# A decode step on one core: the wait for the two final stores moves from SyncE to GpSimd

## The chip, the cores and the metric

The kernel runs on one core of a Trainium2 chip. The metric is the device time in microseconds, the median of several runs. One more execution was taken by the hardware profiler; durations below are from that execution. The engines are called as in the profile: PE (matmuls; PEld its weight loads), DVE (vector), ACT (scalar), POOL (GpSimd) and SP (SyncE). A q behind a name (SPq) marks the engine's sequencer, which issues transfers and waits on semaphores.

## What is computed

One token for each of two batch rows is taken through a normalisation, windowed attention over a cache and a gate from a small dense network:

```
xn = layernorm(x)                                  # 2 x 1 x 448
q = xn @ wq                                        # 16 heads of 256
k, v = last 2048 rows of the caches                # 8 heads, each serves two of q
o = softmax(q k^T / 16) v
s = o @ wo                                         # back to 448
g = silu(relu(xn @ w1) @ w2)
out = x + s * g                                    # 2 x 1 x 448, bf16
```

## The kernel before

A small class, `_Prog`, holds one list of operations for each engine. Every operation names those that it depends on. `op` (L31) adds an engine instruction and `dma` (L38) adds a transfer, issued by the engine named (`e.dma_start`, L39). `run` (L43) then gives each transfer a semaphore of its own, which its completion raises by 16, and each engine one semaphore that its instructions raise by 1 where somebody depends on them. `emit` (L60) writes an engine's list in order; ahead of an operation it writes `eng.wait_ge` (L69) for each semaphore that the operation depends on and that this engine hasn't waited for yet. An operation whose function is `None` is made of its waits alone.

An engine runs its list strictly in order. What each list holds:

- SP issues all the large loads: `wq`, `w1`, `w2`, four tiles of the key cache of 4 MB each, later the value cache into the same four tiles, then `wo` in five parts. At the end it issues the first half of the result.
- ACT issues the three small loads of `x`, then clears accumulators and makes the exponentials; at the end it issues the second half of the result.
- POOL clears small tiles and builds an identity matrix in the first three microseconds (`p_xc`, `i0`, `p_id`, `p_z`, L249 to L269). It has no operation after that, and it issues no transfer.
- DVE transposes the keys within each tile, takes the maxima and turns the probabilities; PE makes the products. Both have jumps written into their code, which set the order in which their code is fetched (`emit_dve`, `emit_pe`).

The four pairs of batch row and head group are worked through in turn: transposed keys, scores, softmax, then the products with the values; the output projection with `wo` closes. At the end, the sum `v_t` (L546) multiplies the projection by the gate, and `v_o` (L548) adds `x` and leaves the result in `out_sb`, four rows from partition 0 and four from partition 32. `d_o` (L550) stores these two halves, the first issued by SP, the second by ACT; each moves 4 rows of 224 bytes to memory. L551 then makes SP wait until both have landed, and L552 makes PE wait for `v_o`. Nothing else follows in any list.

Of the kernel before, what the change touches and what calls it, by code (L numbers as in the profile page):

```python
# [11 lines left out]
PE, DVE, ACTE, SP, POOL = "pe", "dve", "act", "sp", "pool"  # L12
# [121 lines left out]
def bass_recurrent_scan__sliding_block_cached__dense_activation_relu__decode_kernel(  # L134
# [34 lines left out]
    with es:  # L169
        pr = _Prog(nc, es)  # L170
# [70 lines left out]
        def half(t, h):  # L241
            return t.rearrange("b s (k h n) -> h (b s k) n", h=2, n=NCOL)[h]
# [305 lines left out]
        v_o = pr.op(DVE, lambda e: e.tensor_tensor(  # L548
            out=out_sb[0:ROWS, :], in0=tmp[0:ROWS, :], in1=x_c[0:ROWS, :], op=ALU.add), [v_t] + d_xc)
        d_o = [pr.dma(eng, half(out, h), out_sb[32 * h:32 * h + 4, :], [v_o]) for h, eng in ((0, SP), (1, ACTE))]  # L550
        pr.op(SP, None, d_o)  # L551
        pr.op(PE, None, [v_o])  # L552

        pr.run()
# [28 lines left out]
```

## Time and profile before

| | |
|---|---|
| median of three runs | 110.05 us (110.00 to 110.17) |
| the profiled execution's own time | 110.12 us |
| its span, from the first to the last instruction | 108.8 us |
| mean granted TensorE clock | 0.843 |
| bytes read, mean rate | 44.11 MB, 405 GB/s |
| busy: DVE, PE, PEld, ACT, POOL | 61.5, 58.9, 15.7, 9.0, 2.1 us |
| last instruction of POOL | starts at 2.66 us, 0.23 us long |
| last sum (L548) | starts at 107.12 us, 0.27 us long |
| issue of the two stores (L39) | 107.42 us; 0.35 us on SP, 0.27 us on ACT |
| SP's wait for the stores (L69) | 1.0 us |

The span covers the kernel's instructions; the time of an execution also holds what lies around them, here 1.32 us. Waits are not counted as busy. Where a view of the profile names a releaser, it is the operation whose semaphore came last. Line numbers are those of the kernel; since one helper writes all transfers and another all waits, these have the lines of the helpers, L39 and L69.

### The profile page before, as it was taken

To read this page: it belongs to the slowest core of one execution; us is meant where nothing else is said; L and a number is where in the kernel's file an instruction comes from. 1 tells how busy PE (TensorE), PEld (TensorE's weight loads), DVE (VectorE), ACT (ScalarE), POOL (GpSimd) and SP (SyncE) were. 2 spreads that over 40 slices of the span, in tenths; PEclk is the share of its full clock that TensorE was granted. 3 is DMA by queue.
4 is the path that set the end of the run, shared out by engine and by line. 5 is a ranking of instruction groups with operands and counts; after the bars stand their busy time and mean duration, and the time that the engine had idled before them with its cause. 6 is when DMAs were issued, how large, how long until landed. Compare 5 with 4: busy or idle time off the path is not lost.

```text
span 108.8 us, 1117 instructions
## 1 busy us (share of the span) xinstructions
PE 58.9 (54%) x469; PEld 15.7 (14%) x469; DVE 61.5 (57%) x84; ACT 9.0 (8%) x18; POOL 2.1 (2%) x13
## 2 busy tenths in 40 slices
PE   0001295650000069929961995299448967869672
PEld 0000023120000012101200120011033222303131
DVE  2920007644099979999999999940448332204021
ACT  2970000000000000002000200020020000000000
POOL 7000000000000000000000000000000000000000
PEclk9999999995555558995997599679955699999999
DMA  6899999999998999899989998999899899999960
GB/s 165 337 449 390 413 434 486 423 398 494 434 410 386 506 434 410 386 482 458 410 386 482 458 410 386 482 458 410 386 482 458 367 416 428 434 428 448 376 242 1
DMA packets 2487, 44.16 MB, mean 406 GB/s; under 512 B 306, under 2 KB 436, under 8 KB 820
## 3 DMA queue, kind: packets, MB, share of 16 engines
q1 hardware_dynamic: 2456, 44.11, 95.0%
q8 instruction: 3, 0.05, 0.2%
q10 hardware_dynamic: 28, 0.00, 0.0%
HBM read 44.11 MB, written 0.00 MB: 405 GB/s over the span
## 4 chain that ended last, share of the span: by engine, by line
DMA 56%; DVE 28%; PE 8%; SPq 5%; issue 1%
DMA kv<-in_A_k_cache_dram 32%; DVE kv L346 24%; DMA wqo<-in_A_wo_dram 23%; PE sbk L311 7%; SPq L39 5%; PE fbk L311 1%; DVE q_x L375 1%; DVE rm L363 1%; DVE rm_t L365 0%; DVE bias L369 0%; DVE bt L366 0%; DVE tmp L546 0%; DVE out_sb L548 0%
## 5 line engine op out<-in xcount | busy, mean ns | idle before, releaser
L311 PE MATMUL sbk<-kv,qstat 128*8 128x512 bf16 x128 | 30.1, 1086 | 22.8 <-DVE kv L346 22.8
L346 DVE STREAM_TRANSPOSE kv<-kv 128x2048 f32<-128x2048 f32 x16 | 35.6, 2274 | 4.6 <-DMA kv<-in_A_k_cache_dram 4.6
L311 PEld LDWEIGHTS sbk<-kv,qstat 128*8 128x8 bf16 x128 | 5.2, 107 | 46.1 <-DVE kv L346 28.8
L311 PE MATMUL obk<-kv,pt 128*16 128x512 bf16 x128 | 9.5, 441 | 2.6 <-DVE xg L427 1.2
L424 DVE TENSOR_SCALAR o_odd<-obk,rs 128x256 f32<-128x256 f32 x4 | 1.9, 484 | 11.1 <-PE obk L311 11.1
L370 ACT ACTIVATE e_sb<-sbk,bias 128x512 bf16<-128x512 f32 x4 | 2.8, 688 | 51.8 <-DVE bias L369 51.8
L311 PE MATMUL sbk<-kv,f 128*8 128x512 f32 x14 | 7.0, 613 | 0.0
L311 PE MATMUL qbk<-wqo,xr 128*4 128x512 bf16 x28 | 3.2, 626 | 4.2 <-DMA wqo<-in_A_wq_dram 4.2
L363 DVE TENSOR_REDUCE rm<-sbk 128x1 f32<-128x512 f32 x4 | 2.6, 662 | 4.7 <-PE sbk L311 4.7
L311 PE MATMUL mbk<-ident,xg 2*128 2x2 bf16 x7 | 0.3, 161 | 8.4 <-issue 8.4
L329 DVE TENSOR_SCALAR q_x<-qbk 128x512 bf16<-128x512 f32 x1 | 0.7, 691 | 7.2 <-PE qbk L311 7.2
L311 PEld LDWEIGHTS obk<-kv,pt 128*16 128x16 bf16 x128 | 3.2, 97 | 8.7 <-issue 5.0
L375 DVE STREAM_TRANSPOSE q_x<-e_sb 128x512 bf16<-128x512 bf16 x4 | 2.8, 691 | 1.7 <-ACT e_sb L370 1.7
L392 DVE TENSOR_TENSOR pt<-spk,pmask 128x512 bf16<-128x512 f32 x4 | 2.6, 684 | 0.8 <-PE spk L311 0.8
L311 PE MATMUL qbk<-w_sb,xr 128*2 128x448 bf16 x28 | 2.8, 572 | 0.0
L528 DVE COPY wc<-wbk 128x448 f32<-128x448 f32 x1 | 0.6, 624 | 3.8 <-PE wbk L311 3.8
L311 PE MATMUL spk<-q_x,perm 128*32 128x128 bf16 x16 | 0.7, 298 | 3.1 <-DVE q_x L375 3.1
L340 DVE CAST qstat<-mbk 32x256 bf16<-32x256 f32 x4 | 1.7, 420 | 0.7 <-PE mbk L311 0.7
L427 DVE SCALAR_TENSOR_TENSOR xg<-obk,rs,o_odd 128x256 bf16<-128x256 f32 x4 | 1.9, 484 | 0.1
L311 PE MATMUL wbk<-wqo,at 128*2 128x448 bf16 x24 | 1.4, 352 | 1.0 <-DMA wqo<-in_A_wo_dram 1.0
L271 DVE BATCH_NORM_STATS2 st<-x_sb 2x6 f32<-2x448 bf16 x1 | 0.6, 616 | 2.0 <-DMA x_sb<-in_A_x_dram 2.0
L311 PEld LDWEIGHTS sbk<-kv,f 128*8 128x8 f32 x14 | 1.3, 96 | 3.1 <-issue 2.6
(72 smaller groups left out, 33.0 us busy)
## 6 DMA issues: line engine op xcount, KB each, us to landing
kv<-in_A_k_cache_dram SPq DMA_DIRECT2D x4, 4096.0 KB, 39.5
kv<-in_A_v_cache_dram SPq DMA_DIRECT2D x3, 4096.0 KB, 22.1
kv<-in_A_v_cache_dram SPq DMA_DIRECT2D x2, 2048.0 KB, 17.6
wqo<-in_A_wq_dram SPq DMA_DIRECT2D x1, 3584.0 KB, 12.2
w_sb<-in_B_w_dram SPq DMA_DIRECT2D x2, 1568.0 KB, 17.1
wqo<-in_A_wo_dram SPq DMA_DIRECT2D x1, 2240.0 KB, 24.4
wqo<-in_A_wo_dram SPq DMA_DIRECT2D x2, 448.0 KB, 25.2
wqo<-in_A_wo_dram SPq DMA_DIRECT2D x1, 336.0 KB, 25.9
```

What stands on the lines that cost most here:

```text
L39: o = _Op(eng, lambda e: e.dma_start(dst, src), [d for d in deps if d is not None], True)
L271: v_bn = pr.op(DVE, lambda e: e.bn_stats(st6[0:B, :], x_sb[0:B, :]), [d_x])
L311: return lambda e: e.matmul(out_ap, lhsT=lhsT, rhs=rhs, start=start, stop=stop, skip_group_check=True, **kw)
L329: v_q = pr.op(DVE, lambda e: e.tensor_scalar(out=view(q_x, 0, [[256, 8], [128, 2], [1, 32]]), in0=view(qbk, 0, [[64, 8], [1, 2], [2, 32]]) ...
L340: st["q"] = st["mbk"] = pr.op(DVE, lambda e, Q=Q: e.tensor_copy(qstat[32 * Q:32 * Q + 32, 256 * Q:256 * Q + 256], mbk[32 * Q:32 * Q + 32, ...
L346: st["turn", u] = pr.op(DVE, lambda e, n=n: e.transpose(kf[:, 2048 * n:2048 * n + 2048], kf[:, 2048 * n:2048 * n + 2048]), [d_k[u]])
L363: v = pr.op(DVE, lambda e: e.tensor_reduce(out=rm[:, 0:1], in_=sbk[u % 2][:, :], axis=AX.X, op=ALU.max), [last_S[u], p_z, st.get(("rmt", u ...
L370: st["exp", u] = pr.op(ACTE, lambda e: e.activation(e_sb[:, :], sbk[u % 2][:, :], ACT.Exp, bias=bias[:, 0:1], accum_out=ssum[:, u:u + 1]), ...
L375: st["et", u] = pr.op(DVE, lambda e: e.transpose(q_x[:, 512 * u:512 * u + 512], e_sb[:, :]), [st["exp", u], m_qt])
L392: st["pt", u] = pr.op(DVE, lambda e: e.tensor_tensor(out=view(pt[u], 0, [[8, 64], [2, 4], [1, 2]]), in0=view(spk, 128 * u, [[2, 64], [0, 4 ...
L424: v = pr.op(DVE, lambda e: e.tensor_scalar(out=o_odd[:, :], in0=obk[:, DH:2 * DH], scalar1=rs[:, 2 * u + 1:2 * u + 2], scalar2=None, op0=A ...
L427: st["osb", u] = pr.op(DVE, lambda e: e.scalar_tensor_tensor(out=o_sb[:, lo:lo + DH], in0=obk[:, 0:DH], scalar=rs[:, 2 * u:2 * u + 1], in1 ...
```

## The change

The operation that waits for both stores moves from SP's list to POOL's. The stores themselves stay where they are, one issued by SP and one by ACT, and PE's wait stays too.

```diff
         d_o = [pr.dma(eng, half(out, h), out_sb[32 * h:32 * h + 4, :], [v_o]) for h, eng in ((0, SP), (1, ACTE))]
-        pr.op(SP, None, d_o)
+        pr.op(POOL, None, d_o)
         pr.op(PE, None, [v_o])
```

In `run`, this makes `emit` write the waits for the two stores' semaphores as the last of POOL's code, behind the clearing of `at2`, and SP's code ends with the issue of its store.

## The prediction

> **What bounds the kernel, and its end.** I read the page's shares and the chain first, to see whether the change lies where time is spent. The chain that ended last is transfers and vector work from front to back:
>
> ```profile
> span 108.8 us, 1117 instructions
> ...
> DMA 56%; DVE 28%; PE 8%; SPq 5%; issue 1%
> ```
>
> The DMA engines carry 95% of the span (queue q1), and nothing of that is edited. The change is at the tail only, so the second view is the order of time from 106.7 us on (start, length, what):
>
> ```profile
> 107.12 0.27 DVE L548 TENSOR_TENSOR out_sb<-tmp,x_c 36x112 bf16<-36x112 f32 x1
> 107.42 0.35 SPq L39 DMA_DIRECT2D out_dram<-out_sb  x1
> 107.42 0.27 ACTq L39 DMA_DIRECT2D out_dram<-out_sb  x1
> ```
>
> The last sum is ready at 107.39, both stores are issued at 107.42, and nothing is listed after that. Yet the span runs to 108.80: what is left is SP's wait. The third view is what SP waited for, and the fourth the instructions of the wait's line:
>
> ```profile
> SPq L69 <- DMA out_dram<-out_sb: 1.0, 1, 1.0
> ```
> ```profile
> L69 PEldq EVENT_SEMAPHORE  x10: 51/51/4097, 8.3 to 107.4; - x10
> L69 DVEq EVENT_SEMAPHORE  x3: 21/21/50, 3.3 to 106.8; - x3
> L69 SPq EVENT_SEMAPHORE  x1: 192/192/192, 108.6 to 108.6; - x1
> ```
>
> SP's wait is one instruction for both stores' semaphores. Its record starts at 108.604, after the ACT store's last arrival (108.588), and ends at 108.796, 23 ns after the SP store's (108.773). That is the end of the span. The profiled execution took 110.12 us, so 1.32 us lie outside the 108.80; its own 110.12 stands 0.07 above the median of 110.05.
>
> What fills the time behind the span is seen in the trace's list of semaphore updates. The kernel's own semaphores are numbers 99 to 125. Number 2 is not the kernel's; it is raised nine times in each of four groups, here in us from the span's start:
>
> ```
> a  -8.361  -3.592  -2.699  -2.656  -2.632  -2.520  -2.481  -2.447  -2.397
> b  -0.371  -0.336  -0.298  -0.254  -0.231  -0.119  -0.081  -0.046   0.000
> c 107.893 108.048 108.086 108.130 108.923 108.968 109.006 109.040 109.087
> d 109.872 109.906 109.944 109.988 110.012 110.110 110.148 110.183 110.229
> ```
>
> I read each group as a barrier of five engines: five raises one way, four back. Behind group c almost every semaphore from 3 to 255 is touched once between 109.04 and 109.65 (I take it for clearing), then comes group d, and with it the end. So the program's end is the stores' landing, then one engine's wait, then what is left of group c from that engine's place on, then 1.142 us that follow in any case (109.087 to 110.229).
>
> The fifth place is SP: its raise alone is late, 127 ns after SP's wait. The slowest reactions are in the fourth place (43 to 44 ns) and the first (46 to 50 ns, on the way back), and the slowest control instructions are PE's (51 ns) and DVE's (21 ns), so those two places are theirs. The second place was late in c (155 ns behind the first, elsewhere 35): ACT had issued its store until 107.695, while POOL was idle from 2.89 us. So ACT is second and **POOL third**. This is inferred, not recorded.
>
> **The change, step by step.**
>
> *Removed: SP's wait.* SP's last work is then its store issue, over at 107.763. ACT, with its issue over at 107.695, raised 353 ns later, so SP would be ready at about 108.12, well before 108.77. What is late next is the same thing as before, the landing, seen by another engine. Both DMAs are issued by the same engines in the same places, and no queue is moved past.
>
> *Added: POOL's wait.* POOL's last work is the clearing of a tile, over at 2.89 us (2.66 + 0.23); no instruction and no DMA of POOL stands behind the wait, so nothing is queued there but the way out of the program. Its spinning for 105 us replaces spinning at the barrier, which I cost at nothing. The wait instruction itself: in the group of the launch line,
>
> ```profile
> L568 POOLq EVENT_SEMAPHORE  x2: 17/17/17, 0.5 to 0.6; - x2
> ...
> L568 POOLq DRAIN  x1: 186/186/186, 0.3 to 0.3; - x1
> ...
> L568 SPq EVENT_SEMAPHORE  x1: 17/17/17, 0.7 to 0.7; - x1
> ```
>
> both take 17 ns. POOL's one wait in the first microseconds reacted 24 ns after the raise (semaphore 125 at 1.077, instruction at 1.101), SP's 17 (0.637 to 0.654): 7 ns more.
>
> *From POOL's wait to POOL's raise (X).* The trace has no row, since POOL was at the barrier 105 us early. Rows near it: SP 127 ns after its wait; PE 414 after its wait (107.479 to 107.893); ACT 353 after its issue. From the barrier's last own raise to the first clearing, the third place needs 147 ns (109.006 to 109.153) and the fifth 120 (108.923 to 109.043): 27 more. POOL's DRAIN took 186 ns against 7 of SP's, but 136 of it lay beside its memsets (the last ended at 0.440, the DRAIN at 0.490). The least is the third place's bare reaction, 38 ns, the most PE's 414. PE is the slow one in all such rows, and POOL goes with SP in the others, so I take SP's 127 plus the 27, and a little for a DRAIN: **160 ns**.
>
> The Trainium skill (Advanced Engine Details and Errata, Clock Domains) gives the sequencers of SP and POOL the same 1.2 GHz. By that alone X would be SP's 127 and the sum 0.14 us; the two 17 ns rows agree, the 147 against 120 does not.
>
> *From POOL's raise to the barrier's end.* Now the third place is the late one. The trace has that very case in group a: -2.699 to -2.397, 302 ns. Groups b and d, with nobody late, need 298 and 285 from there. SP late costs 164 (108.923 to 109.087). The difference is more than the two places forth and back: with SP late the fourth place answers in 45 ns, in the other groups in 98 to 112, as it has only just raised itself. I take 300.
>
> The Trainium skill (Runtime: NRT & Kernel Launch, The ~15µs preamble/postamble breakdown) describes this barrier as a walk of eight hops of 44 ns. Whole groups b and d, 371 and 357 ns, agree with its 355. By its hop, six hops instead of four would add 88 ns where the rows give 136, and the sum would be 0.13; the rows decide.
>
> *Sum.* Before: landing to barrier's end 23 + 127 + 164 = 314 ns. After: (23 + 7) + 160 + 300 = 490. The difference is **+0.176 us**, on the profiled execution 110.30, on the median 110.05 + 0.18 = **110.23**. Ends: X = 38 with 285 gives 353, or +0.04; X = 414 with 302 gives 746, or +0.43. Were POOL in another place, the way from there would change it: fourth -0.04, second +0.04, first +0.07.
>
> A measurement of this kernel can tell about 0.2% (0.22 us) from no change; the three runs shown spread from 110.00 to 110.17. The forecast is thus a small loss inside that bound.
>
> **The rivals.**
>
> 1. *Slower, by POOL's way out.* If POOL leaves the program as ACT or PE does (353 or 414 ns) rather than as SP, the sum is +0.37 to +0.43: 110.42 to 110.49. It decides from X = 204 ns on: (30 + X + 300) - 314 = 220. For it: two of the three measured ways are that long, and POOL's DRAIN was the longest of all engines. Against: PE's control instructions take three times SP's, ACT's way follows a DMA issue, and POOL's rows lie by SP's.
>
> 2. *Nothing moves.* The places in the barrier matter less than I read, or the time that is counted ends elsewhere: 110.05. For it: the time's bounds are in no view. Against: group d ends 1.43 us behind the span, and 1.32 are counted there.
>
> 3. *A little faster.* The SP store lands 185 ns behind the ACT store (108.773 against 108.588) though issued 5 ns earlier. If SP's waiting behind its own issue holds up that store, it lands with ACT's once SP is free: 0.176 - 0.185 = -0.01, and with X = 38 about -0.14, so 109.91 to 110.04; only with the runs' scatter of 0.08 would that pass 0.2%. Against: the issue itself was 73 ns longer (347 against 274), and a waiting sequencer has no row in which it slows a transfer.
>
> **How the numbers follow.** Forecast (X from 38 to 204) 0.52; rival 1 0.38; rival 2 0.04; rival 3 0.06, of which 0.04 past the bound. So faster 0.04, same 0.52 + 0.04 + 0.02 = 0.58, slower 0.38. The forecast's own range is 110.09 to 110.27. The range for 8 in 10 takes in rival 1's upper end, 110.49, and the low end of X less half the scatter, 110.04; rival 3, most of it, and what is above PE's X are left out.
>
> **What would show it.** The span of the changed kernel should end with a wait of line 69 on POOL, within some 10 ns of 108.80 if the last sum comes at the same time; the span alone should hardly move, and the loss should be in the time around it (1.32 to about 1.50). In the list of semaphore 2, the third raise of group c should be the late one, X behind POOL's wait, with about 300 ns from there to the ninth, and the last two groups 0.78 us apart as before. Wrong would be: the late raise in another place, X near 400, or stores whose two landings draw together.

## The result, and the profile after

The changed kernel takes **110.72 us** (median of 6 runs, 110.55 to 111.01) against 110.09 (6 runs, 110.00 to 110.36): the ratio is 1.0055, 95% interval 1.0040 to 1.0071. It is slower by 0.6 us. I had forecast +0.18 and a range that ended at 110.49.

What the profile shows of the kernel hardly changed. Here are the same two lines of the page, of the changed kernel:

```profile
span 108.9 us, 1117 instructions
...
DMA 56%; DVE 28%; PE 8%; SPq 5%; issue 1%
```

The order of time at the end (start, length, what) is the old one too, 0.05 us later:

```profile
107.18 0.27 DVE L548 TENSOR_TENSOR out_sb<-tmp,x_c 36x112 bf16<-36x112 f32 x1
107.47 0.35 SPq L39 DMA_DIRECT2D out_dram<-out_sb  x1
107.47 0.28 ACTq L39 DMA_DIRECT2D out_dram<-out_sb  x1
```

And the waits (L69; count, shortest, median and longest ns, first and last start) show the moved one on POOL, with the same 192 ns that it had on SP:

```profile
L69 PEldq EVENT_SEMAPHORE  x10: 51/51/4036, 8.3 to 107.5; - x10
L69 DVEq EVENT_SEMAPHORE  x3: 21/21/49, 3.3 to 106.9; - x3
L69 POOLq EVENT_SEMAPHORE  x1: 192/192/192, 108.7 to 108.7; - x1
```

The stores land at 108.642 and 108.828, 186 ns apart (before: 185), and POOL's wait ends at 108.858, which is the end of the span. The profiled execution took 110.71 us, so 1.85 us now lie around the span, where 1.32 did. Of the 0.59 us between these two executions, 0.53 lie behind the last instruction that the profile shows. The medians are 0.63 apart; the other 0.1 us is less than the scatter of the spans (108.7 to 109.2 us in the six runs of the changed kernel), so nothing shows it to belong to the change. The records of semaphore 2 tell where the 0.53 us arise; these are the last two groups, in us:

```
before  c 107.893 108.048 108.086 108.130 108.923 108.968 109.006 109.040 109.087
        d 109.872 109.906 109.944 109.988 110.012 110.110 110.148 110.183 110.229
after   c 108.061 108.104 109.395 109.439 109.462 109.559 109.598 109.634 109.680
        d 110.464 110.498 110.536 110.580 110.604 110.701 110.739 110.774 110.820
```

Before, the fifth raise was the late one; now it is the third. POOL's raise comes 537 ns behind the end of its wait (109.395 - 108.858), where SP's came 127 behind. From there 285 ns lead to the ninth raise (SP: 164), and from the ninth raise to the last 1.140 us (before: 1.142).

### The profile page after: what moved, and what is told of

Its sections match the earlier page's. It is cut to its first block, busy times and chain, and to the rows that moved or that the text cites. A ratio compares the mean times of both kernels' runs of the same rounds, so it can differ in the third digit from the quotient of the medians.

```text
span 108.9 us, 1117 instructions
## 1 busy us (share of the span) xinstructions
PE 58.5 (54%) x469; PEld 15.4 (14%) x469; DVE 61.5 (56%) x84; ACT 9.0 (8%) x18; POOL 2.1 (2%) x13
## 4 chain that ended last, share of the span: by engine, by line
DMA 56%; DVE 28%; PE 8%; SPq 5%; issue 1%
DMA kv<-in_A_k_cache_dram 32%; DVE kv L346 24%; DMA wqo<-in_A_wo_dram 23%; PE sbk L311 7%; SPq L39 5%; PE fbk L311 1%; DVE q_x L375 1%; DVE rm L363 1%; DVE rm_t L365 0%; DVE bias L369 0%; DVE bt L366 0%; DVE tmp L546 0%; DVE out_sb L548 0%
## 5 line engine op out<-in xcount | busy, mean ns | idle before, releaser
L311 PE MATMUL fbk<-w_sb,h_sb 128*2 128x448 bf16 x14 | 0.9, 351 | 1.5 <-issue 1.5
```

The source lines that it names most:

```text
L311: return lambda e: e.matmul(out_ap, lhsT=lhsT, rhs=rhs, start=start, stop=stop, skip_group_check=True, **kw)
```

## The experiments

In each, "the way out" is the time from an engine's last instruction to its raise of semaphore 2. It can be read only where that engine's raise is the late one, since each place but the first also waits for the raise before it. Beside the ratio I give the time around the span, a run's time less its span: the spans spread by half a microsecond or more from run to run, the difference hardly does. It is 1.31 us for the kernel before (mean of 30 runs, standard deviation 0.03; 1.32 and 1.30 in the two later batches), and 1.84 (6 runs) for the changed one.

**Another engine waits.** Three kernels put the wait on ACT, on DVE, and on PE (there in place of PE's own wait for the last sum):

```diff
-        pr.op(SP, None, d_o)
+        pr.op(ACTE, None, d_o)
```

> ACT waits for both stores instead of SP. In the kernel with POOL waiting, POOL raised semaphore 2 537 ns behind its wait (SP before: 127), which I had put at 160. Theory A, the way out is a cost of POOL's own: ACT's raise comes well under 537 ns behind its wait; if as SP's, 127, and with 323 ns from the second place to the barrier's end (group d of the kernel before), the barrier ends 450 ns behind the wait instead of 291, so +0.16 us against before; if as behind its store issue, 353, +0.39. Theory B, any engine but SP needs some 0.5 us: raise about 540 ns behind the wait, +0.57 us.

> DVE waits for both stores instead of SP; it is fourth in the barrier, with 241 ns from its raise to the end (group d of before). Theory A (POOL's own cost): way out like SP's at DVE's slower sequencer, about 160 ns, barrier's end 400 ns behind the wait, +0.11 us against before. Theory B (any engine but SP): about 540 ns, +0.49 us.

> PE waits for both stores instead of SP, and no longer for the last sum. PE is first in the barrier, 357 to 371 ns from its raise to the end. PE's raise came 414 ns behind its wait in the kernel before and 527 in the changed one. Theory A and theory B agree on PE: 410 to 530 ns, barrier's end 770 to 900 behind the wait, +0.50 to +0.62 us against before. Under theory C, that PE's and POOL's ways are long only because something else is still under way at 107.4 to 108 (PE's code was fetched at 105.6), PE's way is short now: 130 to 200 ns, +0.25.

The line of the waits (L69) in the three kernels; the moved wait is the last of its engine in each:

```profile
L69 ACTq EVENT_SEMAPHORE  x1: 191/191/191, 108.7 to 108.7; - x1
```
```profile
L69 DVEq EVENT_SEMAPHORE  x4: 21/36/193, 3.3 to 108.7; - x4
```
```profile
L69 PEldq EVENT_SEMAPHORE  x10: 51/51/4087, 8.3 to 108.5; - x10
```

These waits end at 108.846, 108.915 and 108.691. The first closing group of semaphore 2 in each:

```
ACT  c 108.127 108.960 108.998 109.042 109.066 109.163 109.202 109.237 109.284
DVE  c 108.473 108.507 108.546 109.055 109.078 109.176 109.214 109.250 109.296
PE   c 108.986 109.020 109.058 109.102 109.125 109.223 109.261 109.297 109.343
```

| who waits | way out, ns | from its raise to the ninth, ns | around the span, us | ratio to before (95%) |
|---|---|---|---|---|
| SP (before) | 127 | 164 | 1.31 | |
| ACT | 114 | 324 | 1.49 | 1.0007 (0.9990 to 1.0024) |
| DVE | 140 | 241 | 1.41 | 1.0003 (0.9985 to 1.0021) |
| PE | 295 | 357 | 1.85 | 1.0047 (1.0028 to 1.0066) |
| POOL (changed) | 537 | 285 | 1.84 | 1.0055 (1.0040 to 1.0071) |

The late raise stood in the second, fourth and first place, as inferred in the prediction. Behind a wait, ACT and DVE leave about as fast as SP, and lose only their places: +0.18 and +0.10 us around the span, where +0.16 and +0.11 were expected (the ratios alone can't tell these two from no change). So theory B, that any engine but SP is slow, falls. ACT's 114 ns holds behind a wait only: in the seven traces in which its raise is late behind its store issue, it comes 353 to 355 ns behind that issue. PE's time is in the range expected by A and B, but its way out was shorter than either: its 295 ns belong to a profiled run with 1.68 us around the span, the least of its nine, and the others reach 1.92. Theory C gave +0.25 us; the mean of +0.54 speaks against it, but the one traced run, with the shortest of all PE's ways out, lies between, so for PE it isn't settled.

**Is POOL only cold after 105 us in one wait?** The first try made POOL wait for the last sum first, and then for the stores:

```diff
-        pr.op(SP, None, d_o)
+        pr.op(POOL, None, [v_o])
+        pr.op(POOL, None, d_o)
```

> As the changed kernel, but POOL waits for the last sum first (ends at about 107.45) and then for the stores. Theory A (fixed cost of POOL's way out): nothing changes, raise about 537 ns behind the wait, +0.6 us against before. Theory D, the sequencer is cold after one wait of 105 us: raise 130 to 250 ns behind the last wait, +0.15 to +0.27 us against before.

It did not do what it was to do. The waits came out in another order, first the SP store's, then the two others in one instruction, so POOL was not woken at 107.4:

```profile
L69 POOLq EVENT_SEMAPHORE  x2: 17/30/43, 108.7 to 108.8; - x2
```

The way out was 532 ns, the time around the span 1.85 us, the ratio 1.0066 (1.0046 to 1.0085). It says nothing on a cold sequencer, only that the 537 comes again. The second try gives POOL an instruction to run at 107.5:

```diff
+        warm = named("warm", [128, 5], F32)
...
-        pr.op(SP, None, d_o)
+        pr.op(POOL, lambda e: e.memset(warm[:, :], 0.0), [v_o])
+        pr.op(POOL, None, d_o)
```

> As the changed kernel, but POOL clears a small tile of 128x5 as soon as the last sum is there, at about 107.4 us, and then waits for the stores: this time POOL has run an instruction 1.3 us before its last wait ends. (The kernel in which POOL should be woken at 107.4 by a wait alone did not do that: both its waits ended behind 108.7.) Theory D, POOL is cold after 105 us in one wait: the raise comes 130 to 250 ns behind the wait and the time is 0.15 to 0.27 us above before. Theory A, a fixed cost of POOL's way out: 530 to 540 ns, +0.53 us.

```profile
107.53 0.10 POOL L552 MEMSET warm<- 128x5 f32 x1 [104.64 <-DVE out_sb L549]
```

POOL idled 104.64 us before it, ran it, and 1.07 us later its wait for the stores began to be served (108.705). The way out is 542 ns, around the span 1.86 us, ratio 1.0052 (1.0032 to 1.0071). Theory D falls.

**Does it belong to the wait?** In the next kernel POOL waits for no store but is busy beyond them, while SP waits as before:

```diff
+        for i in range(2):
+            pr.op(POOL, lambda e, i=i: e.memset(q_x[:, 1024 * i:1024 * i + 1024], 0.0), [v_o])
         pr.op(SP, None, d_o)
```

> SP waits for the stores as before; POOL waits for none, but clears two times 128x1024 of a tile that is no longer used from the last sum on, some 0.95 us each, so that its last work ends at about 109.3, behind the stores. Theory A (the way out is long whatever stands before it): POOL's raise comes about 540 ns behind the end of the second clearing, at about 109.85, and the barrier ends 285 ns later. Theory G, the long way belongs to a wait as POOL's last instruction: the raise comes 50 to 250 ns behind the clearing.

```profile
107.75 1.84 POOL L552 MEMSET q_x<- 128x1024 bf16 x2 [104.85 <-DVE out_sb L548]
```

The clearing ends at 109.597 (the last sum was later in this run than expected), POOL raises at 110.109: 512 ns. Theory G falls; the way out is about as long behind a clearing as behind a wait, and a POOL that was busy to the end isn't cold either. Around the span 1.84 us (two runs), but the span itself is longer here by the clearing; ratio 1.0086 (1.0058 to 1.0114).

**Is it a DRAIN?**

```diff
-        pr.op(SP, None, d_o)
+        pr.op(POOL, lambda e: e.drain(), d_o)
```

> As the changed kernel, with one explicit DRAIN of POOL behind the wait for the stores. So far POOL's way out took 537 and 532 ns, ACT's 114, DVE's 140, PE's 295, SP's 127. Theory E, POOL's way out is long because something in it waits for POOL's cores to answer, as a DRAIN does: the DRAIN's own record takes 200 ns or more, and the way out behind it shrinks by about as much if the answer is only slow the first time (cold), or stays at about 535 if every answer costs the same (then the time is 0.2 us or more above the changed kernel). Theory F, the long way is in POOL's instructions behind the kernel and has nothing to do with a DRAIN: the DRAIN takes under 60 ns and the way out stays at 530 to 540.

The one row of the line of this DRAIN:

```profile
L551 POOLq DRAIN  x1: 41/41/41, 109.8 to 109.8; - x1
```

It took 41 ns, and 524 ns of way out follow it (around the span 1.83 us, ratio 1.0037, 1.0013 to 1.0061). Theory E falls for a DRAIN: it is neither slow, nor does one in the kernel save what follows.

**Is it POOL's configuration for the selection?** The identity matrix is replaced by a constant, so that what is made from it has other values; the instructions of the other engines stay.

```diff
-        p_id = pr.op(POOL, lambda e: e.affine_select(
-            out=ident[:, :], in_=ident[:, :], compare_op=ALU.not_equal, fill=1.0,
-            base=0, pattern=[[-1, 128]], channel_multiplier=1), [i0])
+        p_id = pr.op(POOL, lambda e: e.memset(ident[:, :], 0.0078125), [i0])
...
-        pr.op(SP, None, d_o)
+        pr.op(POOL, None, d_o)
```

> As the changed kernel, but POOL's identity matrix is not built: the selection (L265) is replaced by a clearing to one constant, so everything that is made from the matrix is left out of the computation in effect (same instructions elsewhere, other values). With it the two control instructions that stand before the selection in POOL's code (MOVE and MODIFY_POOL_CONFIG, at 1.1 and 1.2 us) should go. Theory H, POOL's long way out undoes that configuration: the raise comes 130 to 250 ns behind the wait. Theory A, the way is POOL's in any program: 510 to 545 ns, time around the span about 1.84 us as in the changed kernel (before: 1.31).

The MOVE and the two MODIFY_POOL_CONFIG are gone from POOL's records; the way out is 543 ns, around the span 1.85 us, ratio 1.004 (1.001 to 1.007). Theory H falls.

**Has the removed half a part in it?** POOL waits, and SP waits too:

```diff
         pr.op(SP, None, d_o)
+        pr.op(POOL, None, d_o)
```

> SP waits for both stores as before, and POOL waits for both as well: the added half of the change alone, without the removed half. If POOL's way out is all that the change costs, this is as slow as the changed kernel, 0.53 us over before, with the raise of POOL again about 537 ns behind its wait. If SP's missing wait had a part in it (a transfer or the store that lands otherwise), the loss is smaller by that part, and the interval between the stores' landings differs.

```profile
L69 SPq EVENT_SEMAPHORE  x1: 191/191/191, 108.7 to 108.7; - x1
L69 POOLq EVENT_SEMAPHORE  x1: 191/191/191, 108.7 to 108.7; - x1
```

Two equal waits, 7 ns apart at their ends (108.898 on SP, 108.905 on POOL). The way out of POOL is 538 ns, around the span 1.88 us, ratio 1.0055 (1.0037 to 1.0073), and the stores land 185 ns apart as ever. The added half alone gives the whole loss (+0.56 us around the span).

**When is it covered?** Two kernels let POOL's wait end earlier; SP waits for both stores in the first, for its own in the second:

```diff
         pr.op(SP, None, d_o)
+        pr.op(POOL, None, [v_o])
```
```diff
-        pr.op(SP, None, d_o)
+        pr.op(SP, None, d_o[:1])
+        pr.op(POOL, None, d_o[1:])
```

> SP waits for the stores as before, and POOL waits for the last sum only (at about 107.45 us). With a way out of 510 to 545 ns POOL would raise at about 107.98, before ACT, the second place, lets it (108.05 to 108.1) and 0.9 us before SP: the whole way out is covered. Expected: no loss, time around the span 1.31 us as before, the fifth raise (SP's) again the late one. If POOL's wait costs by itself, whatever its moment, about 0.5 us are lost.

> The wait is split: POOL waits for the ACT store, which lands some 185 ns before the other, SP for SP's own. With a way out of 530 ns POOL's raise comes 530 behind its wait at 108.60, so at about 109.14, and SP's at 108.92 is hidden behind it; the barrier ends 285 later, at 109.42 instead of 109.087: +0.34 us against before, which is the changed kernel's loss less 0.19. If POOL's way depended on the wait for two semaphores, it is shorter here: +0.1 or less.

The first, then the second:

```profile
L69 POOLq EVENT_SEMAPHORE  x1: 17/17/17, 107.3 to 107.3; - x1
L69 SPq EVENT_SEMAPHORE  x1: 192/192/192, 108.5 to 108.5; - x1
```
```profile
L69 POOLq EVENT_SEMAPHORE  x1: 17/17/17, 108.6 to 108.6; - x1
L69 SPq EVENT_SEMAPHORE  x1: 17/17/17, 108.7 to 108.7; - x1
```

With POOL's wait over at 107.329, the third raise comes 38 ns behind the second, SP's is the late one again (127 ns behind its wait), and 1.33 us lie around the span; ratio 0.9979 (0.9947 to 1.0010), no difference. With the wait over at 108.580, POOL raises at 109.117, 537 ns later, 1.67 us lie around the span (+0.36; expected +0.34), ratio 1.0024 (0.9996 to 1.0052). The loss is what of POOL's way out stands past the other engines, no more. This shows in the time around the span; the ratio of the second kernel alone can't be told from no change.

## Why the prediction was wrong

**The mechanism was right, one term was mis-sized: X, "from POOL's wait to POOL's raise".** I took 160 ns; it is 537. Point by point, on the profiled executions:

| step | predicted, ns | measured, ns |
|---|---|---|
| stores' landing to the end of POOL's wait | 30 | 30 (108.828 to 108.858) |
| POOL's way out, X | 160 | 537 |
| POOL's raise to the barrier's end | 300 | 285 |
| landing to the barrier's end | 490 | 852 |
| the same before | 314 | 314 |
| difference | +176 | +538 |

With X = 537, the prediction's own sum is (30 + 537 + 300) - 314 = +553 ns, against +0.53 us around the span. On the prediction's median of 110.05 that is 110.60, past the end of its range. (That end, 110.49, is a hundredth above its own sum: 110.05 + 0.43 is 110.48.) The rest of its steps held: POOL third (the late raise stands there), nothing queued behind the wait, no change in the stores, 1.14 us behind the barrier, and a span that stays.

Two things went wrong with X. The value was built from SP's 127 and the rows in which POOL's sequencer keeps pace with SP's (17 ns for a wait on both, 147 against 120 ns at the barrier). Those rows tell of single control instructions and single steps of the barrier, and the 17 ns stood again on both engines in the kernel with the split wait; but the way out is a stretch of which no row existed, and it does not follow them: behind a wait ACT 114, SP 127 and DVE 140, against POOL's 512 to 543 in eight traces. That POOL's DRAIN was the longest at the start was no guide either; the same instruction took 41 ns at the end. And the upper end, PE's 414 ns, was one value of one execution: in the thirteen traces (two kernels and eleven variants) PE's way out is 295 to 891 ns. It was the longest of three, not a bound, and the range inherited it.

Rival 1 was right in its direction and its deciding point (X above 204 ns), and too cheap: it gave 110.42 to 110.49. Its lower end was ACT's 353 ns, which belongs to a store issue and not to a wait. Rival 2 falls, since moving the late raise from place to place moves the time. Rival 3 falls: with SP free, the stores land 186 ns apart.

The Trainium skill's walk of 44 ns a hop (Runtime: NRT & Kernel Launch, The ~15µs preamble/postamble breakdown) comes near the part behind the raise: six hops would be 264 ns, 285 were measured. POOL's place cost 121 ns more than SP's (285 against 164), between the 88 that the hops give and the 136 that the prediction took. The Trainium skill's equal clocks for SP's and POOL's sequencers (Advanced Engine Details and Errata, Clock Domains) say nothing of how much each has to do on its way out, and by them the sum was 0.14 us; the measured 537 against 127 decides.

**What stays open** is what fills POOL's way out. It is none of a cold sequencer, the wait, the selection's configuration or an unanswered DRAIN, as far as these runs tell; it lies behind the kernel's last instruction, where the trace has no records but semaphores, and no instruction fetch is recorded in it (the last one in the changed kernel's trace starts at 105.7 us). That excludes little, since no transfer of any kind is recorded behind the stores.

No version here beats the kernel before: SP, fast on its way out and last in the barrier, is the best of the five engines for the last wait here.

## What to carry to other kernels

The program's end isn't the last instruction: each engine still has a way out and a place in a closing barrier, so the engine that finishes last should be the one with the shortest rest. Here, with the last wait on the engine, from the end of the wait to the barrier's end, that is SP (291 ns), then DVE (381), ACT (438) and POOL (822); PE's way out varied too much to count on. An engine with a long way out costs nothing if its last work ends early enough, as POOL's did at 107.3 us. And where a term has no row at all, the range should not end at the longest of a few rows of other engines.

## What the runs showed of the hardware that was not expected

- POOL's way out is nearly constant, 512 to 543 ns in eight traces, behind a wait, a clearing or a DRAIN.
- ACT's way out depends on what it did last: 114 ns behind a wait, 353 to 355 ns behind its store issue.
- PE's way out varies most, 295 to 891 ns, in kernels whose PE code is the same but for its last wait; it was covered everywhere except where PE itself held the last wait.
- A wait for two semaphores is one record that starts when the first is satisfied and lasts until the second is: 192 ns with both stores on one engine, 17 ns each when split over two. Nearly all of that length is the distance of the two landings (185 to 186 ns), not a cost. Where both semaphores had been raised before it began (POOL's second wait in the first try to wake it, raises at 107.332 and 108.525, start at 108.800), it took 43 ns.
